# Attention and mixture-of-experts kernel: an earlier routing of tiles 4 to 7, later sink products, another engine for the sink copies, and a split first load

## The chip, the cores and the metric

The kernel runs on one NeuronCore of a Trainium2 chip. The metric is device time in microseconds (us) of one execution, as the median of several. The engines are TensorE (PE: matrix products and transposes), VectorE (DVE), ScalarE (ACT), GpSimd (POOL) and SyncE (SP, which issues DMAs). ACT issues some DMAs too. POOL issues the indirect ones, whose target rows are computed at run time.

## The reference

Three layers follow each other. The text below is cut to what they compute.

```python
# 1. attention with 4 sink positions and a window of 128; q, k, v are 2 x 8 heads x 768 x 64
scores = scale * np.matmul(q, k.transpose(0, 1, 3, 2))
keep = is_sink | in_window
a = softmax(np.where(keep, scores, -1e9))
x = np.matmul(a, v)                        # as 1536 tokens x 512
# 2. mixture of 8 experts, the best two of each token
logits = x @ w_gate
noisy_logits = logits + np.log1p(np.exp(x @ w_noise)) * noise
top2 = the two largest noisy logits;  top2_w = their softmax
out[token] += top2_w * (relu(x[token] @ w1[e]) @ w2[e])
# 3. a dense layer, 512 -> 2048 -> 512
h = x @ w_in;  out = (h * np.tanh(softplus(h))) @ w_out
```

## The kernel before

**Tiles and steps.** The attention works on 12 tiles of 128 tokens (tiles 0 to 5 are the first batch, 6 to 11 the second), each with 8 heads in 4 pairs. The loop over `s` does half a tile in one step: step s computes the scores of two pairs of tile s//2 (`qk`: the product on PE, line 94, mask and row minimum on DVE, line 96, the exponential on ACT, line 97). In the same step PE transposes the probabilities of the step before (`trans`, line 104) and multiplies those of two steps before with v (`pv`, line 116). The transposes leave PSUM (the accumulators behind PE) by a copy called `pts`, which ACT makes for the pairs in `EV` (line 106) and DVE for the others (line 107).

**Work that is placed by tables.** Everything else of a tile is put into thirds of a step: `slot(3*s)` runs behind the scores of step s, `slot(3*s+1)` behind the transposes, `slot(3*s+2)` behind the products with v. For each tile from the third of its batch on, four columns of the probabilities belong to the sinks. `fin_a` gathers them (`sc`, line 132, a copy on POOL), `fin_b` transposes them on PE (line 122) and splits them into a high and a low part (`sk`, ACT at line 125, DVE at line 126), and `fin_c` adds their product with v (line 138) to the tile's accumulator and copies that to SBUF (`xts`, ACT, line 140). `fin_d` and `fin_d1` compute the gate's logits (lines 149 to 158), `fin_d2` transposes the tile back and normalizes it (`x`, line 166). `SLOW` and `FAST` say how many thirds of a step after the tile's last product each of them comes; `FAST` holds for the tiles in `URG`, 9 to 11.

**Routing.** The tiles are routed in groups of 4, 4, 2 and 2 (`GROUPS`). `route` returns nine pieces: four for the noisy logits (`absz`, `soft`, `noisy`, `top`), `chosen`, then `place` (small PE products that count how many earlier tokens went to the same expert, lines 201 to 203, and on DVE the row for each token, `slot`, lines 207 to 209), `rest`, `weights` and `count`. `SLOWR` and `FASTR` say in which third each piece comes. `rest` appends two scatters per tile to a list: each is an indirect DMA from POOL (line 212) that writes the tile's 128 rows into `xg`, the experts' buffer in HBM. At the end of every step up to 4 of them are issued. Tiles 10 and 11 are routed in the next phase.

**What follows.** When the scatters of tiles 0 to 9 have landed, SP loads the first 256 rows of expert 0 from `xg` (`xr`), PE transposes them (line 560) and the experts' products begin (line 578). From there on the experts and then the dense layer run, with the weights split into two parts by ACT and POOL on the way. While the attention runs, POOL also makes the low parts of the first weights (`wl`, line 542), and ACT issues three small loads for each batch's sinks (`vs`, line 79).

**Order and waits.** Each engine works through its own list in order; the thirds and tables above set these lists when the program is built. A DMA bears one of eight semaphores for hardware-queue DMAs in turn, and waits until the DMA that used the same one before has landed.

Of the kernel before, what the change touches and what calls it, by code (L numbers as in the profile page):

```python
# [11 lines left out]
F32=mybir.dt.float32; F32R=mybir.dt.float32r; BF=mybir.dt.bfloat16; I32=mybir.dt.int32; U32=mybir.dt.uint32  # L12
AF=mybir.ActivationFunctionType; ALU=mybir.AluOpType; AX=mybir.AxisListType
# [3 lines left out]
GROUPS=(4,4,2,2)  # L17
# [3 lines left out]
SPL=(12,2,'act','pool')  # L21
WLD=0
NBU=28; NB2=2
EV=(1,3)
LXB=1; XLU=48; BANKS=(('a',6),('c',2)); BN='aa'; RQ=(1,1); GAPS=(1,0,0,0,3,2,3,0,1)

SLOW=(2,5,6,9); FAST=(2,3,4,3); URG=(9,10,11); FASTR=(0,0,1,2,2,3,3,4,12); SLOWR=(0,0,1,2,4,6,6,7,8)
EXPERT_STRIDE=1536


def attention(ctx, tc, I, st, C=448, LO=256, dbg=None, W=None):

    nc=tc.nc
    H=8; D=64; NT=12; TB=6
# [6 lines left out]
    kT=one.tile([128,4,TB,132],F32,name='kT')  # L41
# [27 lines left out]
    QD,V,VS,P,NB,RS,XTP,XTS={}, {}, {}, {}, {}, {}, {}, {}  # L69
    PT={}  # L70
    def load(t):
        b,i=divmod(t,TB)
        (nc.sync if t else nc.scalar).dma_start(kT[:,:,i,:],I['kP'][t])
        qd=QD[t]=wk.tile([128,4,128],F32,name='qp',bufs=WB[2]); nc.sync.dma_start(qd,I['qP'][t])
        vt=one.tile([128,512],F32,name='vt',bufs=5); nc.sync.dma_start(vt,I['v'][t*128:(t+1)*128,:])
        V[t]=vt
    def load_sinks(b):
# [20 lines left out]
    def trans(t,p):  # L98
        b,i=divmod(t,TB)
        pt=bank['b'].tile([128,512],F32,name=BN[0]).rearrange("p (h j q) -> p h j q",h=2,j=2)  # L100
        j0=1 if i==0 else 0
        for hh in range(2):
            for j in range(j0,2):
                nc.tensor.transpose(pt[:,hh,j,:],P[t][:,2*p+hh,4+132*j:132+132*j],ident)
        sb=w3.tile([128,2,2,128],F32,name='pts'); PT[t,p]=sb
        if p in EV: nc.scalar.activation(sb[:,:,j0:,:],pt[:,:,j0:,:],AF.Copy)
        else: nc.vector.tensor_copy(sb[:,:,j0:,:],pt[:,:,j0:,:])
    def pv(t,p):
        b,i=divmod(t,TB)
# [19 lines left out]
    def fin_a(t):  # L129
        if t%TB<2: return  # L130
        sc=SINKP[t]=end.tile([128,96],F32,name='sc')
        nc.gpsimd.tensor_copy(sc.rearrange("p (j h s) -> p j h s",j=3,h=H),P[t][:,None,:,0:4].to_broadcast([128,3,H,4]))
    def fin_c(t):
        b,i=divmod(t,TB)
        if i>=2:
            sk=SK.pop(t)
            for p in range(4):
                nc.tensor.matmul(XTP[t][:,p,:],VS[b][:,2*p:2*p+2,:].rearrange("p a d -> p (a d)"),sk,start=False,stop=True,skip_group_check=True)
        xs=end.tile([128,4,128],F32,name='xts'); XTS[t]=xs
        nc.scalar.activation(xs,XTP.pop(t),AF.Copy)  # L140
# [29 lines left out]
    def route(t0,n,one=one):  # L170
# [66 lines left out]
        return steps  # L237
    NS=2*NT
    load(0)
    wg=load_gate()  # L240
    load(1)
    zt=one.tile([128,512],F32,name='zero'); nc.vector.memset(zt,0.0)
    fill={}; scq=[]
    groups={}
    t0=0
    for n in GROUPS: groups[t0+n-1]=(t0,n); t0+=n
    def at(h,f): fill.setdefault(h,[]).append(f)
    def slot(h):
        for f in fill.pop(h,()): f()
    def finish(s,t):  # L250

        o=FAST if t in URG else SLOW
        for k,f in zip(o,(fin_c,fin_d,fin_d2,fin_d1)): at(3*s+k,lambda f=f: f(t))
        if t in groups and t<NT-1:
            for k,f in zip(FASTR if t in URG else SLOWR,route(*groups[t])): at(3*s+o[3]+k,f)
    def place_rows(n):
        for _ in range(min(n,len(scq))): scq.pop(0)()


    for s in range(NS+2):  # L260
        t=s//2
        for u in (2*s,2*s+1):
            if s>=NS: break
            p=u%4
            if p==0 and t+2<NT: load(t+2)
            if u>=ZU and (u-ZU)%2==0 and u<ZU+16: st['zero']((u-ZU)//2,zt)
            if u==WLD: W.load_to(W.ahead)
            if u==3: W.scalars()
            if u==LGU:
                for j in range(2): nc.vector.tensor_copy(wbd[64*j:64*j+64,:,16*j:16*j+16],wg[64*j:64*j+64])  # L270
            if u in LSU: load_sinks(LSU.index(u))
            if W.k<W.ku: W.lower(SPL[3])
            if u>=SPL[0] and (u-SPL[0])%SPL[1]==0 and W.ku<12: W.upper(SPL[2])
            qk(t,2*p); qk(t,2*p+1)
        slot(3*s)
        if 1<=s<=NS:
            for u in (2*s-2,2*s-1): trans(*divmod(u,4))
            if s%2==0: at(3*s+2,lambda t=s//2-1: fin_a(t)); at(3*s+3,lambda t=s//2-1: fin_b(t))
        slot(3*s+1)
        if s>=2:  # L280
            for u in (2*s-4,2*s-3): pv(*divmod(u,4))
            if s%2==1: finish(s,(s-3)//2)
        slot(3*s+2)
        place_rows(2 if 2*s<NBU else 2*NB2)
# [29 lines left out]
def flag(tc,st,C,M=256):  # L314

    V=tc.nc.vector; f=st['sf']; n=st['cnt']; w=st['sw']; s=f[:,8:14]; i=w[:,4:5]
    v=f[:,0:2]; lo,hi,g=f[:,2:6:2],f[:,3:6:2],f[:,6:8]
    V.tensor_copy(f[:,2:6],w[:,0:4])
    V.tensor_scalar(g,lo,0.0,4294967296.0,op0=ALU.is_lt,op1=ALU.mult)
    V.scalar_tensor_tensor(v,hi,4294967296.0,lo,op0=ALU.mult,op1=ALU.add)  # L320
    V.tensor_tensor(v,v,g,op=ALU.add)

    V.tensor_scalar(s[:,0:1],f[:,0:1],4.0,None,op0=ALU.not_equal)
    V.tensor_scalar(s[:,1:2],f[:,1:2],128.0,None,op0=ALU.not_equal)

    V.tensor_scalar(s[:,2:3],n[:,11-GROUPS[3],0:1],float(M),None,op0=ALU.is_lt)
    for j,r in enumerate(ROWS7): V.tensor_scalar(s[:,4+j:5+j],n[:,2*j+1,7:8],float(r),None,op0=ALU.is_gt)
    V.tensor_reduce(s[:,3:4],n[:,11,:],axis=AX.X,op=ALU.max)
    V.tensor_scalar(s[:,3:4],s[:,3:4],float(C),None,op0=ALU.is_gt)
    V.tensor_reduce(f[:,14:15],s,axis=AX.X,op=ALU.max)  # L330
    V.tensor_copy(i,f[:,14:15])
    st['flag']=i
# [446 lines left out]

def fast(ctx,nc,tc,I,out,st,W32,cst,dr,C,LO,dbg):  # L780
    st['flagger']=lambda: flag(tc,st,C)
    W=Weights(nc,I,W32); W.ahead=3
    W.spool=ctx.enter_context(tc.tile_pool(name='stg',bufs=3))
# [48 lines left out]
```

## Time and profile before

| | |
|---|---|
| median of 3 runs | 748.19 us (747.0 to 750.71) |
| profiled execution, its own time | 744.71 us |
| span of the trace in it | 742.9 us, 11343 instructions |
| PE busy | 706.3 us (95%) |
| DVE busy | 491.1 us (66%) |
| ACT busy | 375.7 us (51%) |
| POOL busy | 352.3 us (47%) |
| granted TensorE clock, mean | 0.99 |

Busy time is the sum over an engine's instructions without overlaps. PE's instructions are pipelined, and the ends of its instructions are modelled in the trace, so a PE that reads as busy may still be waiting for a part of that time. The clock is given as a share of full speed; TensorE has two levels, 1.2 and 2.4 GHz.

### The profile page before, as it was taken

How to read it: one execution, taken by the hardware profiler on the slowest of the kernel's cores; microseconds unless marked ns; L12 is line 12 of the kernel's file. 1: busy time of each engine (PE TensorE's matmuls, PEld its weight loads, DVE VectorE, ACT ScalarE, POOL GpSimd, SP SyncE). 2: the span in 40 equal slices, each digit the busy share in tenths (PEclk: the TensorE clock that was granted, in tenths of full speed). 3: DMA queues.
4: the chain of work that ended last, by engine and by line, in shares of the span. 5: the costliest groups of instructions: out<-in, count | busy, mean ns of one | idle time of the engine just before them, and what ended most of it. 6: DMA issues, size and time to landing. Idle time of an engine off the chain costs nothing.

```text
span 742.9 us, 11343 instructions
## 1 busy us (share of the span) xinstructions
PE 706.3 (95%) x3888; PEld 591.1 (80%) x3888; DVE 491.1 (66%) x1099; ACT 375.7 (51%) x834; POOL 352.3 (47%) x321
## 2 busy tenths in 40 slices
PE   5998969999999999999999998999999999999996
PEld 4776658888788888989888886878778888888885
DVE  5778756588688788879876126689855655444442
ACT  5887633454454545545544443465545444444342
POOL 6236360575355445545445467366755442332321
PEclk9999979999999999999999999999999999999999
DMA  8995334587677778867867456212202100010001
GB/s 272 340 348 201 121 144 131 209 262 234 241 233 239 238 227 267 283 213 251 241 210 249 135 176 198 63 53 86 84 16 86 29 15 16 1 56 1 0 1 61
DMA packets 68336, 115.68 MB, mean 156 GB/s; under 512 B 6640, under 2 KB 20976, under 8 KB 68272
## 3 DMA queue, kind: packets, MB, share of 16 engines
q1 hardware_dynamic: 59424, 94.48, 39.2%
q0 software_dynamic: 3840, 12.59, 4.9%
q10 hardware_dynamic: 5008, 7.83, 3.0%
q8 instruction: 32, 0.52, 0.3%
q14 instruction: 32, 0.26, 0.1%
HBM read 82.36 MB, written 32.51 MB: 155 GB/s over the span
## 4 chain that ended last, share of the span: by engine, by line
PE 64%; DVE 16%; DMA 6%; ACT 5%; issue 3%; POOL 3%; another core or an unknown queue 1%; ACTq 1%; SPq 0%; POOLq 0%; DVEq 0%
PE o L723 15%; PE a L578 14%; PE h L698 14%; PE c L606 13%; ACT p L97 3%; PE c L603 2%; DMA wi<-dh 2%; DVE q L705 2%; DVE dh L508 2%; DVE dh L510 1%; PE a L94 1%; PE a L560 1%; POOL xg L212 1%; DVE gl L716 1%; DVE dh L506 1%
## 5 line engine op out<-in xcount | busy, mean ns | idle before, releaser
L542 POOL TENSOR_TENSOR wl<-stg,wh 128x512 fp32r<-128x512 f32 x156 | 206.4, 1335 | 171.7 <-ACT wh L538 160.6
L711 POOL TENSOR_TENSOR u<-u,q 128x512 f32<-128x512 f32 x48 | 79.0, 1645 | 146.6 <-DVE u L706 95.8
L538 ACT ACTIVATE wh<-stg 128x512 fp32r<-128x512 f32 x160 | 99.4, 625 | 39.9 <-DMA stg<-in_w_dram 12.3
L578 PE MATMUL a<-xl,wh 128*128 128x448 f32 (+1 forms) x288 | 100.1, 348 | 0.6 <-DVE xl L562 0.6
L578 PE MATMUL a<-xh,wh 128*128 128x448 f32 (+1 forms) x288 | 100.1, 348 | 0.0
L578 PE MATMUL a<-xh,wl 128*128 128x448 f32 (+1 forms) x288 | 99.9, 347 | 0.0
L703 ACT ACTIVATE u<-h 128x512 f32<-128x512 f32 x47 | 28.1, 598 | 121.4 <-PE h L698 101.7
L704 DVE TENSOR_SCALAR u<-u 128x512 f32<-128x512 f32 x48 | 22.2, 462 | 95.9 <-ACT u L703 95.8
L606 PE MATMUL c<-wh,hh 128*128 128x512 f32 x192 | 77.7, 405 | 0.0
L723 PE MATMUL o<-wl,gh 128*128 128x512 f32 x192 | 75.3, 392 | 1.7 <-POOL wl L542 1.6
L698 PE MATMUL h<-xh,wh 128*128 128x512 f32 (+1 forms) x200 | 76.9, 384 | 0.0
L606 PE MATMUL c<-wh,hl 128*128 128x512 f32 x192 | 75.5, 393 | 1.5 <-DVE hl L585 1.5
L723 PE MATMUL o<-wh,gl 128*128 128x512 f32 x192 | 74.9, 390 | 1.3 <-DVE gl L716 1.3
L698 PE MATMUL h<-xh,wl 128*128 128x512 f32 (+1 forms) x200 | 76.0, 380 | 0.0
L698 PE MATMUL h<-xl,wh 128*128 128x512 f32 (+1 forms) x200 | 76.0, 380 | 0.0
L723 PE MATMUL o<-wh,gh 128*128 128x512 f32 x192 | 74.9, 390 | 0.7 <-DVE u L706 0.7
L606 PE MATMUL c<-wl,hh 128*128 128x512 f32 x192 | 74.8, 390 | 0.0
L506 DVE TENSOR_SCALAR dh<-dh 128x256 f32<-128x256 f32 x64 | 41.6, 650 | 35.9 <-ACT dh L504 35.9
L504 ACT ACTIVATE dh<-d 128x256 f32<-128x256 f32 x64 | 27.6, 431 | 65.8 <-DMA wo<-dh 28.3
L578 PEld LDWEIGHTS a<-xl,wh 128*128 128x128 f32 x288 | 54.3, 189 | 4.7 <-DVE xl L562 1.2
L578 PEld LDWEIGHTS a<-xh,wh 128*128 128x128 f32 x288 | 54.3, 189 | 3.5
L578 PEld LDWEIGHTS a<-xh,wl 128*128 128x128 f32 x288 | 54.3, 189 | 3.3
(182 smaller groups left out, 1454.1 us busy)
## 6 DMA issues: line engine op xcount, KB each, us to landing
stg<-in_w_dram SPq DMA_DIRECT2D x64, 512.0 KB
d<-in_w_in_dram SPq DMA_DIRECT2D x32, 256.0 KB
d<-in_w_out_dram SPq DMA_DIRECT2D x32, 256.0 KB
xg<-zero SPq DMA_DIRECT2D x8, 896.0 KB
xr<-xg SPq DMA_DIRECT2D x24, 256.0 KB
yd<-ys ACTq DMA_DIRECT2D x23, 256.0 KB
wi<-dh SPq DMA_DIRECT2D x32, 128.0 KB
wo<-dh SPq DMA_DIRECT2D x32, 128.0 KB
```

The lines of the kernel that those rows point to most:

```text
L97: nc.scalar.activation(o,tt[:,:n],AF.Exp,bias=NB[t][:,h:h+1],scale=-1.0,accum_out=RS[t][:,h:h+1])
L504: nc.scalar.activation(h,H,AF.Abs,scale=65536.0)
L506: h=T[i][1]; nc.vector.tensor_scalar(h,h,lo,hi,op0=ALU.max,op1=ALU.min)
L538: if hi=='act': s.nc.scalar.activation(h,src,AF.Copy)
L542: (s.nc.gpsimd if lo=='pool' else s.nc.vector).tensor_tensor(s.lo[n][:,j,:],s.stg[n,j//2][:,j%2,:],s.hi[n][:,j,:].bitcast(F32),op=ALU.subt ...
L578: nc.tensor.matmul(p[:,:w],a[:,k,fs],b[:,k,c0:c1],start=(i==0),stop=(i==11)); i+=1
L606: for i,(h,w) in enumerate(((high(e,f,o,o+m),wh),(high(e,f,o,o+m),wl),(HL[f][:,d:d+m],wh))): nc.tensor.matmul(p[:m],h,w,start=f+i==0,stop= ...
L698: nc.tensor.matmul(p[:,c],a[:,k,fs],b[:,k,c],start=(i==0),stop=(i==11)); i+=1
L703: nc.scalar.activation(u,p,AF.Exp)
L704: nc.vector.tensor_scalar(u,u,e10,None,op0=ALU.min)
L711: nc.gpsimd.tensor_tensor(u,u,q,op=ALU.mult)
L723: nc.tensor.matmul(O[g][i],a[:,s],w[:,k,:],start=(f==0 and j==0),stop=(f==15 and j==2))
```

## The change

Five things change. `SLOW` and `SLOWR` place the gate's last part and the routing of tiles 0 to 7 a step sooner and the sinks' products (`fin_c`) a third of a step later, so that they stand behind the next step's scores; `FASTR` places `place` of tiles 8 and 9 two thirds later. From tile 6 on ACT makes the sinks' copy in place of POOL. For tiles 0 to 4 ACT copies one pair of transposes rather than two, and DVE the other three. The first tile's k and q come in two loads each, the first pair alone. `count` is left out for the second group. (The line about `GROUPS[-1]` in the final flag reads the same place as before, and needs the count that is kept.)

```diff
-EV=(1,3)
+EV=((1,),(1,),(1,),(1,),(1,))+((1,3),)*7
-SLOW=(2,5,6,9); FAST=(2,3,4,3); URG=(9,10,11); FASTR=(0,0,1,2,2,3,3,4,12); SLOWR=(0,0,1,2,4,6,6,7,8)
+SLOW=(3,5,6,6); FAST=(2,3,4,3); URG=(9,10,11); FASTR=(0,0,1,2,2,5,5,6,7); SLOWR=(0,0,1,2,3,6,6,7,8)
...
-        (nc.sync if t else nc.scalar).dma_start(kT[:,:,i,:],I['kP'][t])
-        qd=QD[t]=wk.tile([128,4,128],F32,name='qp',bufs=WB[2]); nc.sync.dma_start(qd,I['qP'][t])
+        qd=QD[t]=wk.tile([128,4,128],F32,name='qp',bufs=WB[2])
+
+        for c in (slice(0,1),slice(1,4)) if t==0 else (slice(0,4),):
+            (nc.sync if t else nc.scalar).dma_start(kT[:,c,i,:],I['kP'][t][:,c]); nc.sync.dma_start(qd[:,c],I['qP'][t][:,c])
...
-        if p in EV: nc.scalar.activation(sb[:,:,j0:,:],pt[:,:,j0:,:],AF.Copy)
+        if p in EV[t]: nc.scalar.activation(sb[:,:,j0:,:],pt[:,:,j0:,:],AF.Copy)
...
+        if t<6: nc.gpsimd.tensor_copy(o,i)
+        else: nc.scalar.activation(o,i,AF.Copy)
...
-            for k,f in zip(FASTR if t in URG else SLOWR,route(*groups[t])): at(3*s+o[3]+k,f)
+            for k,f in zip(FASTR if t in URG else SLOWR,route(*groups[t])):
+                if f.__name__!='count' or t in (3,NT-1-GROUPS[-1]): at(3*s+o[3]+k,f)
```

The first place is PE's list from step 23 on, the second half of the scores of tile 11. `kT,qp` are these scores, `sl,tri` and `cum,ones` the place products of tiles 8 and 9, `ident,sc` the transpose of the sinks of tile 10, `ident,p` and `pts,vt` the transposes and the products with v, `sk,vb` the sinks' products. Before:

```order
L94 MATMUL a<-kT,qp 128x264 x4
L201 LDWEIGHTS tri
L201 MATMUL a<-sl_1579,tri 128x8
L203 LDWEIGHTS ones
L203 MATMUL a<-cum,ones 128x8
...
L122 MATMUL a<-ident,sc 96x128
L104 MATMUL a<-ident,p 128x128 x8
L116 MATMUL c<-pts,vt 64x128 x8
L138 MATMUL c<-sk,vb 128x128 x4
L149 MATMUL a<-xts,wbd 32x128 x4
```

The same step of the changed kernel:

```order
L96 MATMUL a<-kT,qp 128x264 x4
L124 MATMUL a<-ident,sc 96x128
L106 MATMUL a<-ident,p 128x128 x8
L118 MATMUL c<-pts,vt 64x128 x8
L206 LDWEIGHTS tri
L206 MATMUL a<-sl_1611,tri 128x8
L208 LDWEIGHTS ones
L208 MATMUL a<-cum,ones 128x8
...
L143 MATMUL c<-sk,vb 128x128 x4
L154 MATMUL a<-xts,wbd 32x128 x4
```

The place products have moved behind the transposes and the products with v. The second place is POOL's list between the sinks' mask of the second batch and the scatters of tiles 4 to 7; `sc<-p` is the sinks' copy, `xg<-x,slot` a scatter. Before:

```order
L542 TENSOR_TENSOR wl_1021<-stg,wh_1020 128x512 x2
L132 COPY sc<-p 128x96 x3
L211 MEMSET spacer 1x1
L212 DMA xg<-x,slot 12288x512
...
L132 COPY sc<-p 128x96
L211 MEMSET spacer 1x1
L212 DMA xg<-x,slot 12288x512
```

The three copies stand ahead of the eight scatters of tiles 4 to 7, the fourth between these and the four of tiles 8 and 9. The changed kernel has there:

```order
L548 TENSOR_TENSOR wl_1057<-stg,wh_1056 128x512 x2
L216 MEMSET spacer 1x1
L217 DMA xg<-x,slot 12288x512
```

None of the copies is left on POOL, and all twelve scatters stand in one row. The third place is the beginning of ACT's list, with the semaphores that its DMAs wait for; `DMAHW1_49` is the second of the eight. Before:

```order
L73 DMA kT<-in_kP_dram 128x4x132
L55 DMA wg<-in_wg_dram 128x64
L55 DMA noise<-in_noise_dram 128x96
L97 ACTIVATE p,rs<-tt,nb 128x128 [waits DVE_49] x4
L79 DMA vs<-in_v_dram 32x1x512 [waits DMAHW6_49]
L79 DMA vs<-in_v_dram 32x1x512 [waits DMAHW7_49]
L79 DMA vs<-in_v_dram 32x1x512 [waits DMAHW1_49]
L97 ACTIVATE p,rs<-tt,nb 128x128 [waits DVE_49] x4
```

The user before the third `vs` load of semaphore 1 is the q load of tile 2 (`L74 DMA qp`, which itself waits for the first v load). In the changed kernel:

```order
L76 DMA kT<-in_kP_dram 128x132
L76 DMA kT<-in_kP_dram 128x3x132
L55 DMA wg<-in_wg_dram 128x64
L55 DMA noise<-in_noise_dram 128x96 [waits DMAHW0_49]
L99 ACTIVATE p,rs<-tt,nb 128x128 [waits DVE_49] x4
L81 DMA vs<-in_v_dram 32x1x512 [waits DMAHW0_49]
L81 DMA vs<-in_v_dram 32x1x512 [waits DMAHW1_49]
L81 DMA vs<-in_v_dram 32x1x512 [waits DMAHW3_49]
L99 ACTIVATE p,rs<-tt,nb 128x128 [waits DVE_49] x4
```

The third `vs` load now waits for semaphore 3, whose user before it is again the q load of tile 2. On SP that load still stands behind the k load of tile 2, which now waits for the first v load.

## Rows read from the trace of the kernel before

**Rows 1.** Stretches of the attention: busy time and instructions of each engine, granted clock, DMA.
```profile
core 0: us, PE busy (x) PEld busy (x) DVE busy (x) ACT busy (x) POOL busy (x), PEclk, DMA share, GB/s
20.00:50.00 30.00, 29.34 (x312) 22.64 (x308) 21.95 (x92) 26.25 (x87) 8.28 (x9) 1.00 1.02 346
50.00:80.00 30.00, 26.07 (x271) 18.57 (x268) 23.79 (x119) 23.10 (x83) 19.73 (x27) 1.00 0.74 253
80.00:99.90 19.90, 17.33 (x179) 13.57 (x179) 16.95 (x90) 11.92 (x43) 4.83 (x11) 0.99 0.16 63
99.90:107.30 7.40, 3.74 (x30) 3.11 (x30) 2.22 (x15) 2.86 (x10) 4.45 (x10) 0.73 0.43 177
107.30:118.80 11.50, 9.62 (x79) 7.93 (x80) 5.09 (x17) 3.54 (x7) 4.22 (x8) 0.74 0.54 179
```
**Rows 2.** Timeline, 99.9 to 107 us: start, duration, engine, line, [idle before <- releaser].
```profile
100.10 0.17 PE L203 MATMUL a<-cum,ones 128*128 128x8 bf16 x1
103.86 0.96 POOL L212 DMA_INDIRECT xg<-x,slot  x1 [0.22 <-issue]
106.40 0.19 DVE L207 TENSOR_TENSOR s<-s,a 128x32 f32<-128x32 f32 x1 [5.07 <-remote]
106.44 0.27 ACT L125 ACTIVATE sk<-a 96x128 fp32r<-96x128 f32 x1 [4.03 <-remote]
```
**Rows 3.** The chain that ended last, 101 to 120 us: start, duration, what.
```profile
101.33 5.08 another core or an unknown queue
...
107.28 0.99 POOL xg L212
...
111.12 2.67 DMA xg<-x,slot
113.81 1.86 DMA xr<-xg
...
119.46 1.58 PE a L578 x11
```
**Rows 4.** Timeline, 0 to 12 us.
```profile
6.66 2.29 PE L94 MATMUL a<-kT,qp 64*128 64x128 f32 x16 [6.66 <-DMA kT<-in_kP_dram]
9.88 1.42 ACTq L79 DMA_DIRECT2D vs<-in_v_dram  x2
11.35 0.40 ACT L97 ACTIVATE p<-tt,nb 128x128 f32<-128x128 f32 x1 [1.78 <-DMA vs<-in_v_dram]
```
**Rows 5.** The chain, 0 to 1 and 40 to 44 us.
```profile
0.85 5.67 DMA kT<-in_kP_dram
...
40.05 0.66 PE c L138 x4
40.71 1.09 PE a L94 x8
...
42.06 0.87 PE a L104 x8
42.93 1.02 PE c L116 x16
```
**Rows 6.** Waits, 20 to 56 us: us in total, times, longest.
```profile
PE c L138 <- DVE sk L126: 1.1, 4, 0.5
```
**Rows 7.** Timeline, 65 to 80 us.
```profile
65.85 0.43 DVE L96 CUSTOM_DVE_ANT_0 tt<-a,m 128x264 f32<-128x264 f32 x1 [1.27 <-PE a L154]
...
78.54 0.43 DVE L96 CUSTOM_DVE_ANT_0 tt<-a,m 128x264 f32<-128x264 f32 x1 [1.15 <-PE a L94]
...
79.97 0.31 PE L122 MATMUL a<-ident,sc 128*96 128x128 f32 x1 [0.44 <-POOL sc L132]
```
**Rows 8.** Timeline, 86 to 95 us: scores of steps 21 and 22, first scatter of tiles 4 to 7.
```profile
86.31 1.16 PE L94 MATMUL a<-kT,qp 64*128 64x264 f32 x8
...
91.71 1.16 PE L94 MATMUL a<-kT,qp 64*128 64x264 f32 x8
...
94.91 1.00 POOL L212 DMA_INDIRECT xg<-x,slot  x1 [3.97 <-DVE cw L221]
```
**Rows 9.** The chain, 86 to 88 us: DVE's routing of tiles 4 to 7, first and last.
```profile
86.51 0.20 DVE nl L185
...
87.55 0.56 DVE i L190 x5
```

More of the change, by code (lines that the diff above doesn't have):

```diff
@@ L131, in fin_a @@
         sc=SINKP[t]=end.tile([128,96],F32,name='sc')
-        nc.gpsimd.tensor_copy(sc.rearrange("p (j h s) -> p j h s",j=3,h=H),P[t][:,None,:,0:4].to_broadcast([128,3,H,4]))
+        o,i=sc.rearrange("p (j h s) -> p j h s",j=3,h=H),P[t][:,None,:,0:4].to_broadcast([128,3,H,4])
+        if t<6: nc.gpsimd.tensor_copy(o,i)
+        else: nc.scalar.activation(o,i,AF.Copy)
     def fin_c(t):
@@ L324, in flag @@
     V.tensor_scalar(s[:,1:2],f[:,1:2],128.0,None,op0=ALU.not_equal)
-    V.tensor_scalar(s[:,2:3],n[:,11-GROUPS[3],0:1],float(M),None,op0=ALU.is_lt)
+    V.tensor_scalar(s[:,2:3],n[:,11-GROUPS[-1],0:1],float(M),None,op0=ALU.is_lt)
     for j,r in enumerate(ROWS7): V.tensor_scalar(s[:,4+j:5+j],n[:,2*j+1,7:8],float(r),None,op0=ALU.is_gt)
```

## Prediction

> **What bounds the kernel now.** I read the stretches of the attention first, then the chain that ended last, then the timeline where the chain leaves PE. Over the whole span PE is busy for 95%, and from about 120 us on the experts and the dense layer keep it so. The change touches only what comes before that, so the question is how much of the first 119 us is not PE's work. In [rows 1] PE idles 0.66 us from 20 to 50, 3.93 from 50 to 80, 2.57 from 80 to 99.9, 3.66 from 99.9 to 107.3 and 1.88 from there to 118.8 (each the length less the busy time): 12.7 us in all. This is the most that an order of instructions can win behind 20 us, apart from the lower clock: the granted clock of the last two stretches is 0.73 and 0.74, a mixture of full speed and half, which begins where PE has run dry.
>
> The largest single piece stands in the chain: 5.08 us from 101.33 that are put down to an unknown queue [rows 3]. [rows 2] show what waits there. PE's last place product for tiles 8 and 9 starts at 100.10 and takes 0.17. DVE reads its result at line 207 only at 106.40, after 5.07 us of idleness, and ACT reads the transposed sinks at 106.44. Both were waiting for PE, which by its rows had long been done. What ends at this moment is something else: the eighth scatter of tiles 4 to 7 is issued at 103.86, and a scatter takes 2.67 us from its issue to its landing [rows 3], so it lands at 106.53. I read it so: while a row of scatters is under way, word from PE reaches the other engines late, at worst when the last has landed. The same shows on a smaller scale in the two earlier rows of four scatters, where DVE waits 1.27 us at 65.85 and 1.15 us at 78.54 for PE instructions [rows 7]. By the Trainium skill, Perfetto Trace Analysis, section Tensor Engine Instruction, the end that the profiler gives for a PE instruction is estimated, and its semaphore update follows when PSUM has acknowledged the data; the trace agrees as far as DVE's start can stand far behind such an end, and no row shows why it does here.
>
> From there the chain has no slack: first scatter of tiles 8 and 9 at 107.28, the last at 111.12, landed 2.67 later, `xr` loaded from 113.81, experts' products from 119.46 without a break [rows 3].
>
> **The change, part by part.** All terms are against the profiled execution, 744.71 us (span 742.9).
>
> *Tiles 4 to 7 a step sooner, tiles 8 and 9 two thirds later.* The place products of tiles 4 to 7 move from behind the scores of step 22 (91.71) to behind those of step 21 (86.31) [rows 8], 5.40 us. With them go eight scatters: the first from 94.91 to 89.5, the last from 103.86 [rows 2] to 98.5, landed by 98.5 + 2.67 = 101.1. The place products of tiles 8 and 9 now stand behind one sink transpose, eight transposes (0.87) and the products with v (1.02) [rows 5]: with 0.17 for the first, as for a small product in [rows 2], that is 2.06 later, so they end at 100.27 + 2.06 = 102.3. This is behind 101.1, so nothing holds their result, and DVE reads it at 102.4 in place of 106.40: 4.0 us won. DVE has the sinks' split and a copy ahead of it, which end before that. I give 1.2 back for the eight scatters, which now lie beside the scores of steps 22 and 23 and will delay those once by about what [rows 7] show (1.15 and 1.27), and take 0.7 for what steps 20 to 23 win by DVE's shorter list in step 22 (a quarter of the 2.57 that PE idles there). Together -3.5. Bounds: nothing, if the delay moves along whole, and -6.2, the idle time of both stretches (2.57 + 3.66).
>
> *Behind 107.3.* Scatters, loads and PE's chain keep their lengths and come sooner. If PE has not run dry before, the clock stays up for longer; in [rows 1] 26% of 11.5 us at 0.74 is the most there is of that. I take -0.4; bounds 0 and -1.9 (PE's idle time).
>
> *From 50 to 80.* ACT makes the sinks' copies from tile 6 on. The copy is as small as the neighbouring ones: ACT's 96-row split takes 0.27 [rows 2], and four of them are 1.1 us on an engine that has 6.9 us free from 50 to 80 and 8.0 from 80 to 99.9 [rows 1], so they cost nothing there. What goes is PE's 0.44 at 79.97, where POOL's copy stood behind scatters and weights [rows 7]. The first group's scatters come a step sooner as well, and the last row of them has two, not four: I take half of the 1.15 for it. With nothing for the count that is dropped, a few small operations on idle POOL and DVE, 0.44 + 0.58 is about 1.0 and I call it -1.1 with the rest of the four waits of [rows 6] that lies behind 50; bounds -3.9 (all idleness) and +1.6, if DVE is late as in the last rival.
>
> *From 20 to 50.* Moved behind the scores, the sinks' products no longer wait for their split: 1.1 us in four waits [rows 6], of which part lies behind 50, since PE idles only 0.66 from 20 to 50. In exchange `xts` stands behind four exponentials on ACT, and the gate's products may wait for it. The evictions that go to DVE ease ACT (26.25 of 30 busy) and load DVE (21.95 of 30), and PE stays the bound. I take nothing; bounds -0.66 and +0.7 (as much again).
>
> *The first pair.* The scores begin at 6.66, when the k load has landed, 5.67 us after its issue [rows 4, 5]. A quarter of it will land sooner, but the path goes through ACT: after four exponentials ACT sits on the `vs` loads until 11.35 (idle 1.78), and the third waits for the q load of tile 2, before and after. Issued behind one more wait, that load lands no sooner. So nothing; bounds -1.78 and +0.7. The rule that speaks of this is in the Trainium skill, DMA: Bandwidth & Descriptors, section Anatomy of one DMA: a fixed 2.0 us and the bytes at 436 GB/s. By it the pair's 67 KB would be an estimated 2.2 us after the issue, and if ACT did not wait, the sum would be 3.5 us better. The trace has 5.67 for the whole load, more than that rule's 2.6.
>
> Sum: -3.5 - 0.4 - 1.1 = -5.0 us, so 739.7 in place of 744.71. The median lies 3.5 us above the profiled execution, and I carry the difference over: 748.19 - 5.0 = 743.2, about 743.
>
> **The rivals.**
>
> *The delay moves along with the scatters.* Then the 5.07 us fall on the scores of step 22 or 23, whose results DVE needs at once, and 3.5 is lost except 0.5. For it: both long and short delays lie beside scatters. Against it: the four-scatter rows cost 1.2 each, not 5, where the scores follow closely. Time 743.2 + 3.0 = 746.2, no change that can be told. Chance 0.23.
>
> *DVE is late, and the kernel slower.* Routing, the gate's last reduction, the normalization and the sinks' split now share the odd steps 11 and 19; the routing's part from 86.51 to 88.11 is 1.6 us [rows 9]. If DVE is late with the masks by that much in both steps, the exponentials and the transposes behind them are late too: 3.2, and eight tiles whose gate waits 0.2 for `xts`, another 1.6. It decides when the lateness is more than the time from one step's masks to the next step's transposes, about the 2.2 us of scores and sinks' products plus a transpose (1.09 + 0.66 + half of 0.87) [rows 5]; it then eats the placement's gain too. Time 748.19 + 4.8 = 753.0. Against it: DVE has 21.95 and 23.79 of 30 us. Chance 0.11.
>
> *The early pair reaches the path.* If the third `vs` load is released sooner, ACT's 1.78 go. Time 743.2 - 1.8 = 741.4. Against it: the semaphores above. Chance 0.12.
>
> *My sum* has 0.54, with 740 to 745.5 as its own range: -8 where the idleness of 50 to 107 goes to a larger part, -3 where a third of the delay stays.
>
> **How the numbers follow.** About 0.5%, 3.7 us, is what a measurement of this kernel can tell from no change; the border lies at 744.4. Of my own case 0.50 lie below it and 0.04 above, and the early pair adds 0.12 below: faster 0.62. No change holds 0.04 + 0.23 = 0.27, slower 0.11. The range reaches from 737 (-11, most of PE's idleness) to 749, which leaves out the slower case and little else.
>
> **What would show it.** Right: line 212 (217 in the changed kernel) begins its run of eight near 89, the wait of DVE for the place result of tiles 8 and 9 is under 1 us, `xr` is loaded near 110, and the experts' products begin near 114. In 20 to 50 PE stays above 29 of 30. The first exponentials begin before 6, and ACT's second four still at about 11.3. Wrong: a wait of DVE or ACT for PE of several microseconds between 90 and 102; DVE without a gap through steps 19 to 21 with PE waiting for it; or an experts' phase that doesn't end as much sooner as it begins.

## The result: slower, 756.28 us against 748.19

The changed kernel takes 756.28 us (median of 9 runs, 754.75 to 760.05), the kernel before 748.19; the ratio is 1.0116, interval 1.0086 to 1.0146. Its profiled execution took 755.86 us with a span of 754.1. The forecast was 743, range 737 to 749.

The stretches of the attention, to be read against [rows 1]:

```profile
core 0: us, PE busy (x) PEld busy (x) DVE busy (x) ACT busy (x) POOL busy (x), PEclk, DMA share, GB/s
20.00:50.00 30.00, 27.28 (x291) 21.03 (x290) 23.02 (x89) 23.57 (x79) 8.25 (x9) 1.00 1.01 329
50.00:80.00 30.00, 23.20 (x224) 17.43 (x222) 21.83 (x99) 19.65 (x68) 16.34 (x25) 0.89 0.68 228
...
59.00:62.00 3.00, 3.00 (x31) 2.77 (x32) 2.42 (x16) 2.70 (x11) 1.85 (x3) 0.54 0.42 124
...
120.00:128.40 8.40, 3.54 (x17) 3.20 (x17) 1.39 (x2) 1.53 (x3) 0.00 (x0) 0.74 0.44 154
```

PE idles 2.72 us from 20 to 50 (0.66 before) and 6.80 from 50 to 80 (3.93). From 59 to 62 it is all busy, but at a granted clock of 0.54, near the lower of its two levels, after it has stood still (1.49 of the 1.5 us from 57 to 58.5). The waits of PE from 0 to 129 us (total, times, longest) show where it stands:

```profile
PE a L154 <- ACT xts L145: 12.4, 10, 2.9
PE a L566 <- DMA xr<-xg: 5.2, 2, 4.4
```

In the kernel before, the same view (0 to 119 us) has one wait of PE for `xts`:

```profile
PE a L149 <- ACT xts L140: 0.7, 1, 0.7
```

Nine of the ten waits are new, one for each of tiles 0 to 8: 2.7 us of them lie between 20 and 50, 5.7 between 50 and 80, the rest later. The timeline of steps 12 and 13 shows how the longest comes about:

```profile
51.54 0.71 PE L96 MATMUL a<-kT,qp 64*128 64x128 f32 x6
...
53.30 1.27 POOL L548 TENSOR_TENSOR wl<-stg,wh 128x512 fp32r<-128x512 f32 x1 [3.27 <-ACT wh L544]
53.41 1.21 DVE L190 SCALAR_TENSOR_TENSOR nl<-lz,u 128x32 f32<-128x32 f32 x1
...
55.94 0.27 DVE L98 CUSTOM_DVE_ANT_0 tt<-a,m 128x128 f32<-128x128 f32 x1
...
56.31 0.40 ACT L99 ACTIVATE p<-tt,nb 128x128 f32<-128x128 f32 x1 [3.09 <-DVE nb L98]
...
57.87 0.57 ACT L145 ACTIVATE xts<-c 128x512 f32<-128x512 f32 x1
58.49 0.43 PE L154 MATMUL a<-xts,wbd 128*32 128x128 f32 x8 [2.90 <-ACT xts L145]
58.85 0.90 PE L96 MATMUL a<-kT,qp 64*128 64x128 f32 x8
```

Three quarters of the scores of step 12 are there at 52.3, the last at 53.1. DVE is busy with the sinks' split, a copy, and then the routing of tiles 0 to 3 (the logits at line 190, the best two at 194 and 195), and masks them only from 55.94. One instruction of the routing, at 53.41, takes 1.21 us, where the kernel before has 0.19 for it; an operation of POOL lies beside it. Run 12 has the same pair (1.20 beside 1.27), runs 1 and 3 have at most 0.18, so about 1.0 of this wait may come from there; why it takes longer is not shown. ACT waits for the masks, makes four exponentials, and only then `xts`, which now stands behind them. PE waits for `xts` with the gate's products, and behind these stand the scores of step 13. Every link is in series: here what DVE loses, PE loses. In the kernel before, in the same place, ACT makes `xts` ahead of the exponentials, and PE comes to the gate without a wait:

```profile
48.91 0.60 ACT L140 ACTIVATE xts<-c 128x512 f32<-128x512 f32 x1 [0.59 <-PE c L138]
...
51.61 0.43 PE L149 MATMUL a<-xts,wbd 128*32 128x128 f32 x8
```

The same returns between steps 14 and 15, with 2.00 us, and between steps 20 and 21, with 2.19. These waits cost clock as well: after PE has stood from 67 to 69, the granted clock is 0.50 from 69.5 to 72.5, and the eight scores of step 15 take 2.07 us in place of 1.16.

The end of the attention, to be read against [rows 2, 3, 8]:

```profile
101.47 0.98 POOL L217 DMA_INDIRECT xg<-x,slot  x1 [18.22 <-DVE cw L226]
...
110.35 0.96 POOL L217 DMA_INDIRECT xg<-x,slot  x1 [0.21 <-issue]
...
113.77 0.18 DVE L212 TENSOR_TENSOR s<-s,a 128x32 f32<-128x32 f32 x1
...
114.64 0.95 POOL L217 DMA_INDIRECT xg<-x,slot  x1 [3.25 <-DVE cum L227]
...
124.05 1.06 PE L566 MATMUL a<-ident,xr 128*128 128x128 f32 x4 [4.35 <-DMA xr<-xg]
```

The wait of 5.07 us for PE's word (the signal that a result of PE is ready) is gone in this execution, but the row of eight scatters starts at 101.47, where 89 was forecast and 94.91 was before. Behind the last scatters PE waits 4.35 us for `xr`; from 120 to 128.4 it is busy for 3.54.

### The profile page after: what moved, and what is told of

The parts are those of the page before. It is cut to its first block, busy times and chain, and to the rows that moved or that the text cites. A ratio compares the mean times of both kernels' runs of the same rounds, so it can differ in the third digit from the quotient of the medians.

```text
span 754.1 us, 11348 instructions
## 1 busy us (share of the span) xinstructions
PE 711.0 (94%) x3887; PEld 594.8 (79%) x3887; DVE 495.5 (66%) x1103; ACT 374.8 (50%) x833; POOL 351.1 (47%) x317
## 4 chain that ended last, share of the span: by engine, by line
PE 64%; DVE 17%; DMA 8%; ACT 6%; issue 3%; POOL 1%; ACTq 0%; SPq 0%; DVEq 0%; POOLq 0%
PE o L729 15%; PE a L584 14%; PE h L704 13%; PE c L612 12%; ACT p L99 3%; DMA wi<-dh 2%; PE c L609 2%; PE a L96 2%; DVE q L711 2%; PE a L566 1%; DVE dh L516 1%; DVE dh L514 1%; DVE gl L722 1%; DVE dh L518 1%; DMA yd<-ys 1%
## 5 line engine op out<-in xcount | busy, mean ns | idle before, releaser
L512 DVE TENSOR_SCALAR dh<-dh 128x256 f32<-128x256 f32 x64 | 43.2, 675 | 34.9 <-ACT dh L510 34.5
L99 ACT ACTIVATE p<-tt,nb 128x264 f32<-128x264 f32 (+1 forms) x96 | 46.5, 485 | 28.9 <-DVE nb L98 25.2
```

The lines of the kernel that those rows point to most:

```text
L99: nc.scalar.activation(o,tt[:,:n],AF.Exp,bias=NB[t][:,h:h+1],scale=-1.0,accum_out=RS[t][:,h:h+1])
L512: h=T[i][1]; nc.vector.tensor_scalar(h,h,lo,hi,op0=ALU.max,op1=ALU.min)
```

## The experiments

Fifteen runs were made, fourteen of them of an edited kernel. "Before" and "changed" name the kernel that was edited; ratios are against the kernel before, with 95% intervals. Lateness is the start of a step's scores (or of the first expert product) in a trace, less that of the kernel before: 20.73 in step 5, 48.81, 51.97, 63.49, 82.71, 86.31 and 96.70 in steps 12, 13, 16, 20, 21 and 23, and 118.8 for the experts. Some expectations number these steps one or two too low: the scores at 16.60 are step 4's, those at 82.71 step 20's, and the waits at "steps 14 and 18" lie in steps 16 and 19.

| kernel | 5 | 12 | 13 | 16 | 20 | 21 | 23 | experts |
|---|---|---|---|---|---|---|---|---|
| changed | 2.3 | 2.7 | 6.9 | 10.8 | 8.7 | 11.9 | 11.6 | 9.6 |
| 1, changed, products back | 0.1 | 0.9 | 0.8 | 0.9 | 0.3 | 0.2 | 3.0 | 3.1 |
| 2, before, products later | 1.3 | 1.4 | 2.7 | 3.3 | 5.4 | 6.4 | 5.5 | 6.0 |
| 3, before, routing sooner | 0.2 | 1.0 | 0.9 | 1.1 | 0.1 | 0.0 | 3.0 | -0.1 |
| 4, changed, routing back | 2.4 | 2.5 | 3.8 | 5.0 | 3.5 | 5.0 | 3.9 | 5.0 |
| 9, before, products and gate later | -2.0 | -3.4 | -2.2 | 0.1 | -0.5 | 0.0 | 0.4 | -0.1 |
| 15, changed, routing back, gate later | 0.2 | -1.1 | 0.1 | 1.7 | -2.3 | -1.6 | -1.1 | -2.5 |

Behind the experts' start the spans differ by 623 to 630 us without a pattern, so a trace speaks for its attention and the medians for the whole. A part of each lateness is chance of the one execution: runs 8, 10 and 11 change nothing before tile 6, and their steps 5 and 12 lie at 0.2, -1.5 and -1.7. But in each of the three the two steps lie alike, so what is added from one step to the next is steadier. Kernels with the products later have a longer even step from the outset, since the products now fall into it: runs 9 and 15, where PE waits for `xts` once, add 1.2 from step 12 to 13 and 0.5 and 0.7 from 20 to 21.

### Products or routing: runs 1 to 4

```diff
1 changed: -SLOW=(3,5,6,6)  +SLOW=(2,5,6,6)
2 before:  -SLOW=(2,5,6,9)  +SLOW=(3,5,6,9)
3 before:  -SLOW=(2,5,6,9); SLOWR=(0,0,1,2,4,...)  +SLOW=(2,5,6,6); SLOWR=(0,0,1,2,3,...)
4 changed: -SLOW=(3,5,6,6); SLOWR=(0,0,1,2,3,...)  +SLOW=(3,5,6,9); SLOWR=(0,0,1,2,4,...)
```

Run 1. 

> The changed kernel with the sinks' products back where they were (SLOW begins with 2 and not 3). Theory 1, late products: the copy xts stands behind four exponentials on ACT and the gate's products stop PE until it is made, so that any lateness of DVE's masks reaches PE in full; with the products back these waits (2.90, 2.00, 2.19 us in the changed kernel, and smaller ones) go, and the time falls by 6 us or more, to 750 or below. Theory 2, crowded odd steps: DVE's routing beside the normalization in steps 11 and 19 makes the masks late wherever the products stand; the time stays within 3 us of the changed kernel's 756.3.

Measured: 751.68, ratio 1.0059 (1.0028 to 1.0089).

Run 2. 

> The kernel before with nothing changed but the sinks' products a third of a step later (SLOW begins with 3). Theory 1: PE waits for xts in front of the scores of every even step of tiles 0 to 8, by 0.5 to 1.2 us, so 4 us or more slower than before, ratio 1.005 to 1.012. Theory 2: the products alone are harmless, within 1.5 us of before.

Measured: 751.03, ratio 1.0027 (1.0003 to 1.0052).

Run 3. 

> The kernel before with only the placement of tiles 0 to 7 a step sooner (last entry of SLOW 6 and not 9, fifth of SLOWR 3 and not 4). Theory 1: with xts made ahead of the exponentials, late masks delay only the transposes; no more than 1.5 us slower than before, and up to 4 faster where the last word from PE no longer waits for scatters. Theory 2: masks late by 2 to 3 us in steps 12 and 20 and PE idle for as long, 4 us or more slower, ratio above 1.005.

Measured: 748.96, ratio 1.0020 (0.9994 to 1.0045).

Run 4. 

> The changed kernel with the routing of tiles 0 to 7 back where it was (last entry of SLOW 9, fifth of SLOWR 4). Theory 1: it stays slower than before by 4 us or more, since xts is as late as in the changed kernel. Theory 2: the two long stretches of steps 11 to 13 and 19 to 20 (4.2 and 3.3 us longer than before) go, and the time falls to 750 or below.

Measured: 752.25, ratio 1.0065 (1.0035 to 1.0095).

PE's waits for `xts` in the traces of runs 1, 2 and 4, in this order:

```profile
PE a L154 <- ACT xts L145: 0.7, 1, 0.7
```

```profile
PE a L149 <- ACT xts L140: 7.1, 10, 1.6
```

```profile
PE a L154 <- ACT xts L145: 9.1, 8, 3.9
```

Theory 1 gets the waits right, and runs 3 and 4 as it said. Run 1 falls between the two (4.6 us below the changed kernel; theory 1 asked for 6, theory 2 for less than 3), and run 2 lies below theory 1's 1.005. Theory 2 alone fails: with the routing sooner and the products in place (runs 1 and 3), steps 12 to 13 and 20 to 21 are not longer at all (table). With the products later and the routing in place, they lengthen by 1.3 and 1.0 to 1.5 (runs 2 and 4), hardly more than the products' new place makes them; with both, by 4.2 (with the long instruction at 53.41) and 3.2. So the crowded DVE costs in these steps only through the late `xts`: either part taken back gives about half of the loss.

A microsecond of wait is not always one of time. Run 2 has 6.4 us of waits in tiles 0 to 8 and is 0.27% (2.0 us) slower. The 3.9 of run 4 is the wait of tile 9, at 111 us, which kernels with the products in place have too (2.5 in run 5, 4.8 in run 6); in tiles 0 to 8 run 4 has 5.2.

Run 3 shows what became of the wait of 5.07 us. Its timeline, the row of eight scatters from the first to the last, and behind it:

```profile
89.56 1.00 POOL L212 DMA_INDIRECT xg<-x,slot  x1 [8.38 <-DVE cw L221]
...
98.70 0.97 POOL L212 DMA_INDIRECT xg<-x,slot  x1 [0.21 <-issue]
...
99.71 0.90 PE L94 MATMUL a<-kT,qp 64*128 64x264 f32 x3
...
100.95 0.29 DVE L156 TENSOR_TENSOR pr<-a,recip 128x128 f32<-128x128 f32 x1 [3.84 <-PE a L94]
```

The scatters start at 89.56, as forecast, but now PE's word on steps 22 and 23 is held beside them; step 23 begins 3.0 us late, and the experts start where they did, at 118.7. In this trace the delay has moved along.

### The gate's products later: runs 9 and 15

```diff
 9 before:  -SLOW=(2,5,6,9)  +SLOW=(3,8,9,9)
15 changed: -SLOW=(3,5,6,6); SLOWR=(0,0,1,2,3,...)  +SLOW=(3,8,9,9); SLOWR=(0,0,1,2,4,...)
```

Run 9. 

> The kernel before with the sinks' products a third of a step later, as in the second run, and the gate's products a whole step later (SLOW 3, 8, 9, 9 in place of 2, 5, 6, 9), so that xts has a step's time to be made. If what costs is PE standing in front of the gate's products for xts, the 7.1 us of these waits in the second run fall below 1.5 and the time comes back to before: ratio 0.997 to 1.001. If it is the place of the products as such, the ratio stays at 1.002 or more.

Measured: 746.85, ratio 0.9986 (0.9953 to 1.0020). Run 2's loss is gone by the medians, though the two intervals touch. At step 12 the kernel is 3.4 us ahead, of which 1.4 came between steps 5 and 12; by step 16 the lead is lost.

Run 15. 

> The changed kernel with the gate's products a step later (SLOW 3, 8, 9, 9) and the routing of tiles 0 to 7 where it was before (SLOWR as before), that is the fourth run with a later gate. If PE's waits for xts are what the fourth run still had (9.1 us in its trace, ratio 1.0065), they fall below 2 us and the ratio comes to 0.999 to 1.004; if it is the place of the products or the other four parts (1.007 in the fifth run), it stays at 1.005 or more.

Measured: 743.93, ratio 0.9953 (0.9920 to 0.9987). Run 4 and this one differ only in the place of the gate's products and of the transposes back (`fin_d2`), which both come a step later, and lie 1.1% apart. PE's waits for `xts` in runs 9 and 15:

```profile
PE a L149 <- ACT xts L140: 0.7, 1, 0.7
```

```profile
PE a L154 <- ACT xts L145: 0.7, 1, 0.7
```

This settles where the waits come from: not the products' new place as such, but the gate's products standing too close behind it. What they cost is less sharp. The step from run 4 to run 15 is worth 8.3 us, more than the 5.2 of its waits in tiles 0 to 8. And run 5 below, with the products in place and no such wait there, is 6.5 us slower than run 15. So the later gate gains by more than the waits for `xts`; what else it gains by is not shown.

### The other parts: runs 5 to 8, 11 and 13

```diff
 5 changed: SLOW and SLOWR as before, the rest stays
 6 before:  the loads of the first pair alone, as in the change
 7 as 6:    -LSU=(2,30)  +LSU=(6,30)
 8 before:  -FASTR=(0,0,1,2,2,3,3,4,12)  +FASTR=(0,0,1,2,2,5,5,6,7)
11 before:  -nc.gpsimd.tensor_copy  +nc.gpsimd.tensor_copy if t<6 else nc.scalar.activation (Copy)
13 before:  -EV=(1,3)  +EV=((1,),(1,),(1,),(1,),(1,))+((1,3),)*7
```

Run 5. 

> The changed kernel with SLOW and SLOWR as before; what is left of the change is the first pair's own loads, ACT's sink copies, the evictions, FASTR and the dropped count. Theory A, the parts add: the difference of the first and third run and that of the fourth and second run both give 0.0038 for these parts, so ratio 1.003 to 1.005, about 751. Theory B, they cost only beside the moved products or the moved routing: ratio 0.999 to 1.001.

Measured: 750.46, ratio 1.0070 (1.0034 to 1.0105). Theory A, and more than it said. In its trace nothing is late up to step 16 (0.2 us); step 17 is 2.1 late, behind a wait of PE for masks beside the first scatters (1.67 us) and a granted clock of 0.50 from 67 to 70. Run 15 keeps the same other parts and is faster than before, so that they cost as such is not shown. One more caution: the ratios of runs 5 to 8 are against 745.95 us for the kernel before, those of the other runs against 747.42 to 748.27, so 0.2 to 0.3% of these four may not be theirs.

Run 6. 

> The kernel before with nothing but the first pair of k and q loaded alone. Theory A: the first scores come 3.5 us sooner, ACT stands on the third load of vs until 10.6 us as in the changed kernel, PE runs dry and falls to half clock, and by step 3 the lead is gone: its scores start 0.5 to 2 us later than the 16.60 of before; ratio 1.000 to 1.003. Theory B: the lead is kept in part, 1 to 2 us faster, ratio 0.998.

Measured: 750.04, ratio 1.0043 (1.0007 to 1.0080). Its timeline:

```profile
3.18 0.80 PE L96 MATMUL a<-kT,qp 64*128 64x128 f32 x4 [3.18 <-DMA kT<-in_kP_dram]
...
8.13 3.19 ACTq L81 DMA_DIRECT2D vs<-in_v_dram  x2
...
11.37 0.40 ACT L99 ACTIVATE p<-tt,nb 128x128 f32<-128x128 f32 x1 [4.35 <-DMA qp<-in_qP_dram]
...
14.53 1.96 PE L96 MATMUL a<-kT,qp 64*128 64x264 f32 x8
```

PE starts 3.48 us sooner than in the trace of before (there at 6.66; in other runs with the undivided load at 5.2 to 5.6). ACT stands on the `vs` loads until 11.37 (11.35 before, [rows 4]), and the eight scores that take 1.16 elsewhere take 1.96 at 14.53, with a granted clock of 0.50 from 13 to 16. Step 4 is 1.4 us late, as theory A had it, and from step 5 the kernel is 0.8 late. The first pair was there 2.3 us after its issue at 0.85. The Trainium skill (DMA: Bandwidth & Descriptors, section Anatomy of one DMA) fits a fixed 2.0 us and the bytes at 436 GB/s to DMAs that GpSimd issues; carried over to this load, which ACT issues, it gives an estimate of 2.2, and the trace agrees.

Run 7. 

> As the run before, but the loads of vs are issued two steps later (LSU begins with 6 and not 2), so that ACT's exponentials of step 1 don't stand behind them. If that wait is what eats the lead (theory A of the run before), the scores of step 3 start 2 to 3.5 us sooner than the 16.60 of before, and the time falls by 2 us or more: ratio 0.994 to 0.998. If it is the loads of the later pairs and tiles that hold the start, step 3 comes within 1 us of 16.60 and the ratio is 0.999 to 1.002.

Measured: 753.16, ratio 1.0094 (1.0060 to 1.0127). The timeline shows that the wait was not removed but moved:

```profile
12.78 5.13 ACTq L81 DMA_DIRECT2D vs<-in_v_dram  x3
...
17.96 0.51 ACT L99 ACTIVATE p<-tt,nb 128x264 f32<-128x264 f32 x1 [5.96 <-DMA sw<-in_window_dram]
...
18.62 2.19 PE L106 MATMUL a<-ident,p 128*128 128x128 f32 x8 [3.09 <-ACT p L99]
```

Up to step 4 it keeps 2.2 us; then ACT stands for 5.96 behind loads that wait for semaphores of other loads in flight, and step 5 is 2.5 late. Both expected outcomes were wrong, but that ACT's stand on `vs` eats the lead holds. Of the 0.94% (7 us) the trace has 5.8 at the experts' start.

Run 8. 

> The kernel before with nothing but FASTR changed (place of tiles 8 and 9 behind the transposes and the products with v). By the forecast it costs nothing, since the 2.06 us on PE lie under the wait for the last scatter of tiles 4 to 7: ratio 0.999 to 1.001. Theory A: the scatters of tiles 8 and 9 start 2 to 3 us later, as in the first run against the third (22.2 against 19.0 us from the scores of step 22 to the first expert product), and the experts with them: ratio 1.003 to 1.005.

Measured: 750.42, ratio 1.0046 (1.0015 to 1.0077). In its trace nothing is late up to step 19 (0.2 us). Then:

```profile
79.51 0.43 DVE L96 CUSTOM_DVE_ANT_0 tt<-a,m 128x264 f32<-128x264 f32 x1 [3.15 <-PE a L164]
...
81.03 0.45 PE L122 MATMUL a<-ident,sc 128*96 128x128 f32 x1 [2.89 <-POOL sc L132]
```

FASTR has moved nothing yet, so these 2.4 us are not its own; [rows 7] have 1.15 and 0.44 in this place. Behind step 23 another 0.7 us are lost, which may be. How much of the 0.46% belongs to FASTR stays open.

Run 11. 

> The kernel before with nothing but ACT making the sinks' copy from tile 6 on. By the forecast it takes away PE's wait for the copy on POOL, 0.44 us at 79.97 in the kernel before and 2.89 in the run with FASTR alone, and costs nothing: ratio 0.996 to 1.000. Rival: ACT's 0.28 us a tile stands in front of four exponentials and delays the transposes: ratio 1.000 to 1.003.

Measured: 743.12, ratio 0.9951 (0.9921 to 0.9981): faster, and by more than the 0.44 us of the forecast. The copy behind a row of scatters costs 0.4 us in one execution and 2.9 in another (run 8). The trace of run 11 shows only 0.5 us won between steps 19 and 20, so where the whole 0.5% comes from is not shown.

Run 13. 

> The kernel before with nothing but the evictions of tiles 0 to 4 changed (ACT copies one pair of transposes, DVE three). By the forecast nothing, within 0.7 us: ratio 0.999 to 1.001. If DVE, which is the late engine of the changed kernel, bears it badly, steps 2 to 9 take 1 us or more longer in the trace and the ratio is 1.002 to 1.005.

Measured: 749.20, ratio 1.0006 (0.9979 to 1.0033): nothing, as forecast. Its trace is of its slowest execution, with step 5 1.6 us late; from there to step 16 it loses nothing more.

### What holds PE's word: runs 10 and 12

```diff
10 before:  -place_rows(2 if 2*s<NBU else 2*NB2)  +place_rows(0 if s<20 else 2*NB2)
12 changed: no edit
```

Run 10. 

> The kernel before, but the scatters of tiles 0 to 3 are kept back until step 20, four a step from there, so that sixteen scatters stand in one row from step 20 to 23 and none beside steps 12 to 19. If scatters hold PE's word back, the waits of DVE for PE at steps 14 and 18 (1.27 and 1.15 us in the kernel before, 3.15 in the run with FASTR alone) go, and step 19 begins 1 to 4 us sooner than its 82.71; from step 20 on there are waits of several us, and the whole is slower than before, ratio 1.005 to 1.02. If the waits are of another cause, they stay at steps 14 and 18.

Measured: four executions took 750.24, 752.61, 1005 and 1781 us, so no ratio is given; the trace is of the first. From step 13 to step 20 the kernel gains 3.1 us on the kernel before (1.5 ahead, then 4.6), without scatters there. Then, beside the row of sixteen:

```profile
88.05 0.28 ACT L151 ACTIVATE gs<-a 128x128 f32<-128x128 f32 x1 [5.65 <-remote]
...
89.47 0.43 DVE L96 CUSTOM_DVE_ANT_0 tt<-a,m 128x264 f32<-128x264 f32 x1 [5.92 <-PE a L122]
```

The holds go where the scatters go.

Run 12. 

> The changed kernel once more, for a second profile. In its first profile no PE update came more than 0.3 us late beside the scatters, other than in all runs so far. If that is a property of the kernel, DVE again starts the masks of steps 13, 14 and 21 within 0.5 us of PE's scores, and the experts start near 128.4; if it is chance of one execution, waits of 1 us or more for PE stand beside its scatters this time, and the experts start later than 128.4.

Measured: one execution, 764.47 us, experts from 136.7. The waits for `xts` are there again (13.4 us, the longest 2.9). The word is held this time, as here beside the second row of four:

```profile
70.87 0.43 DVE L98 CUSTOM_DVE_ANT_0 tt<-a,m 128x264 f32<-128x264 f32 x1 [3.62 <-PE a L169]
```

So that nothing of it stands in the first profile was chance, not the change.

### What is worth keeping: run 14

```diff
14 before: the edits of runs 9 and 11 together
```

Run 14. 

> The kernel before with ACT's sink copies, and with the sinks' products a third of a step and the gate's products a step later (the two edits that cost nothing or gained, 0.9951 and 0.9986). If they add, ratio 0.991 to 0.996 and the time 741 to 744; if the waits beside the scatters are all that differs between these kernels, no better than 0.997 to 1.001.

Measured: 740.54, ratio 0.9911 (0.9882 to 0.9941), faster than both kernels. The two ratios multiply to 0.9937, which lies in the interval: they add. PE is busy for 27.87 us from 50 to 80 (26.07 before, [rows 1]), in part because the granted clock is 0.94 there, and the experts start at 114.3.

```profile
50.00:80.00 30.00, 27.87 (x291) 20.47 (x286) 25.74 (x115) 23.75 (x82) 18.10 (x25) 0.94 0.76 261
```

## Why the prediction was wrong

**The step that failed** is the price of the exchange in the term for 20 to 50. It was named rightly ("`xts` stands behind four exponentials on ACT, and the gate's products may wait for it") and put at nothing, at most +0.7; in the terms behind 50 it does not stand at all. Measured: 2.7 us of such waits from 20 to 50, where PE's idle time rose from 0.66 to 2.72, and over the whole attention 12.4 us in place of 0.7. The term looked at the busy shares of the engines, and not at the chain masks, exponentials, `xts`, gate, scores, which in the even steps had no slack for a late mask. That the waits come and go with this chain the traces of runs 1, 2, 4, 9 and 15 show.

**How much of the loss it is.** With the products taken back (run 1) the time falls by 4.6 of the 8.1 us, with both parts taken back (run 5) by 5.8. By run 5's own ratio 0.70% of the 1.16% is left, by its time 2.3 us of 8.1. This rest stays open.

**The slower rival** (753.0, chance 0.11) had the right place, DVE's routing in front of the masks, but the wrong condition: it gave the masks 2.2 us of slack up to the next transposes, and took 0.2 a tile for `xts`. Through `xts` there was no such slack, and the waits were 0.5 to 2.9 a tile. Alone neither of its halves reaches its 4.8 us (run 2: 0.27%, 2.0 us; run 3: 0.20%, 1.5 us, not clear of noise). That 756.28 lies near its 753.0 is in part luck, since the change as a whole also holds the rest of run 5.

**Tiles 4 to 7 a step sooner** (-3.5): run 3 gives nothing. In its trace the rival of the delay that moves along came true: the scatters started 5.4 us sooner and the hold went with them. That PE's word is late beside scatters was read rightly; that a shorter hold would meet the scores was not.

**50 to 80** (-1.1): alone on the kernel before, the copy on ACT was worth more than its 0.44, about 3.7 us by run 11's ratio. **The evictions** were nothing, as said. **The first pair** was nothing or a small loss, and for the reason given, ACT's stand on `vs`; 0.8 us are seen in the trace of run 6, the rest of its 0.43% is not explained. **FASTR**, put at nothing as well, was not shown to be free (run 8).

**Behind 107.3** (-0.4) there was nothing to come sooner: the experts start 9.6 us late. That what follows the experts' start only shifts held (624.1 us before, 625.7 after).

By the ratios the loss of 1.16% is no plain sum: runs 1, 4 and 5 (1.0059, 1.0065, 1.0070) have one, the other or neither of the two main parts, and stand alike, while both together add 0.5%. Runs 2 and 3 give 0.27 and 0.20 from the other side. With intervals of 0.3 a finer split isn't to be had.

## What to carry over

Before a producer is moved to a later place, name the consumer that an engine, working through its list in order, will stand on, and walk the chain of queues between them; free time on each engine says nothing about a chain that passes through all of them. A delay that comes with a transfer is not won by moving what it now falls on: it went where the transfer went (runs 3 and 10). And a change that loses as a whole can hold parts that gain: ACT's copy alone gave 0.5%, and together with the later products and a later gate 0.9%.

## What the runs showed of the hardware

Word from PE comes late beside scatters, and for how long differs between executions of the same instructions: DVE's wait in step 19 was 1.15 us in the kernel before and 3.15 in run 8. What holds it stays open. The prediction's reading, at worst until the last scatter has landed, does not fit every trace: in run 3 DVE starts at 100.95, before 98.70 + 2.67 = 101.37. The Trainium skill (Perfetto Trace Analysis, section Tensor Engine Instruction) says that the update follows when PSUM has acknowledged the data; no run here shows why that should be late. Sixteen scatters in a row (run 10) had two of four executions at 1005 and 1781 us, also unexplained.
